# Four tokens in nine of batch 0's q are loaded first, and the rest follows behind v

## The chip, the cores and the metric

The kernel runs on one core of a Trainium2 chip. The metric is the device time of one execution in microseconds, the median of several runs.

## The reference

```python
def _attn_ref(q, k, v):                    # q, k, v: (8, 8, 576, 64) float32
    def phi(x):
        return np.where(x > 0, x, np.exp(x) - 1.0) + 1.0
    q_p, k_p = (phi(q), phi(k))
    kv = np.einsum('bhsd,bhse->bhde', k_p, v)
    z = np.sum(k_p, axis=2)
    num = np.einsum('bhsd,bhde->bhse', q_p, kv)
    den = np.einsum('bhsd,bhd->bhs', q_p, z)[..., None] + 1e-06
    return num / den

def _moe_ref(x, w_in, w_out, beta):        # x: (4608, 512), d_ff = 2048
    h = x @ w_in
    g = h * (1.0 / (1.0 + np.exp(-beta * h)))
    return g @ w_out
```

Linear attention over 8 batches of 8 heads comes first. Its output, transposed to (4608, 512), goes through a two-matrix layer with a Swish whose slope is beta. phi is computed as min(exp(x), max(x, 0) + 1).

## The kernel before

Work goes batch by batch (576 tokens each). A batch's tokens lie as 64 groups of J = 9 consecutive tokens; heads come in pairs. After transposition they make tiles of 128 rows: tiles t = 0 to 3 hold tokens 2t and 2t + 1 of every group, and tile 4 holds the ninth token (64 rows). Tiles 0 to 3 of a batch make the 512 columns of one pass through the layer. The ninth tokens of all batches are gathered in `xT_tail` and make a ninth pass at the end.

For each batch, in order:

- `phi_exp` (ScalarE), `phi_relu` and `phi_min` (VectorE) make phi of q and k, in two halves `pr`.
- q is transposed on TensorE for batches 0 and 1 (`q_half`, `q_last`, then `q_copy` out of PSUM to `qT`).
- `kv_both` makes k'v with a column of ones that gives z. Batch 0 has its own version: `z_sums`, `kv_first`, `kv_mask`, `zbd`, `dps`.
- `numer` (batch 0: `numer_first`, with the denominators from `denom`) makes num and divides; the result is `xs_sb`. `x_trans` (batch 0: `x_first`) transposes it to `xT`.
- The layer: `h_mm` makes one of 16 blocks `ff` of h in PSUM (`h_ps`), `silu` takes it to `g`; `y_mm(b, t, i)` adds the quarter `i` of the hidden units to tile `t` of y.

Batch 0's first four blocks of h are made tile by tile (`h_first(t)`, 16 matmuls of 128 columns each), as soon as each tile of `xT` is there. Blocks 4 to 15 are made at full width. Batch 0's y is made by 16 `y_mm` calls, and between them the attention part of batch 1 is placed: its q transposes, `kv_both(1)`, `numer(1, t)` and `x_trans(1, t)`. From batch 2 on a later batch's attention is placed inside `h_phase` and `y_fast`, where a product is saved by sums of blocks.

The order on each engine is the order in which the program text issues instructions (`manual_schedule`); each engine works through its own list in order and waits on semaphores. `idle(n)` issues n matmuls on a constant tile and nothing uses their result. `table(func)` makes ScalarE load the table of a function ahead of its use.

Loads: SyncE's queue gets the four halves of batch 0's q and k, float32, into parts of `stage` and `xk[0]` (`x0f`). All else comes through GpSimd's queue, in program order, with conversion to bf16 where the tile is bf16: v of batch 0 (`v0b`), four quarters of `w_in`, `w_out` 0 and 1 (float32, into the memory of `g_sb[1]`), q and k of batch 1, `w_out` 2 (into `stage`), v of batch 1, `w_out` 3, q and k of batch 2. GpSimd starts with a one-element copy `gate` that reads the end of q's first half, so that its loads begin when that half has landed:

```python
load(nc.sync, x0f[0], q, 0, 0, 2)
load(nc.sync, x0f[1], q, 0, 2, 2)
load(nc.sync, x0f[2], k, 0, 0, 2)
load(nc.sync, x0f[3], k, 0, 2, 2)
...
nc.gpsimd.tensor_copy(gate, x0f[0][:, 1, J - 1, D - 1 : D])
```

At most eight of GpSimd's loads are under way: the ninth waits for the first to land, and so on.

Of the kernel before, what the change touches and what calls it, by code (L numbers as in the profile page):

```python
# [16 lines left out]
def kernel(  # L17
# [65 lines left out]
    x3f = xk[0].rearrange("p i j d -> p (i j d)").bitcast(F32)  # L83
    x0f = [
        a.rearrange("p (i j d) -> p i j d", i=2, j=J)
        for a in [stage[:, n * 1152 : (n + 1) * 1152] for n in range(3)] + [x3f]
    ]
    v0b = vf.rearrange("p i j d -> p (i j d)").bitcast(BF16)[:, 0:2304].rearrange(
        "p (i j d) -> p i j d", i=4, j=J
# [6 lines left out]
    ws = [consts.tile([P, 8, HM], BF16, name=f"ws{i}") for i in range(4)] if FAST else None  # L96


    def load(eng, dst, src, b, i0=0, n=4):
        return eng.dma_start(  # L100
            out=dst.rearrange("p i j d -> p i (j d)"),
            in_=src[b].rearrange("(i a) (g j) d -> (a g) i (j d)", a=2, j=J)[:, i0 : i0 + n],
        )


    beta_row = consts.tile([FC, P], F32)
    nc.scalar.dma_start(out=beta_row, in_=moe_beta.rearrange("(c p) -> c p", p=P))
    load(nc.sync, x0f[0], q, 0, 0, 2)
    load(nc.sync, x0f[1], q, 0, 2, 2)
    load(nc.sync, x0f[2], k, 0, 0, 2)  # L110
    load(nc.sync, x0f[3], k, 0, 2, 2)
    nc.vector.memset(warm, 0.5)
    act0 = consts.tile([P, 1], F32, name="act0")
    nc.scalar.activation(act0, warm[:, 0:1], ACTF.Exp)
# [8 lines left out]
    nc.gpsimd.tensor_copy(gate, x0f[0][:, 1, J - 1, D - 1 : D])  # L123
    load(nc.gpsimd, v0b[:, 0:2], v, 0, 0, 2)
    load(nc.gpsimd, v0b[:, 2:4], v, 0, 2, 2)

    w_in_v = moe_w_in.rearrange("(c p) f -> p c f", p=P)
    w_out_v = moe_w_out.rearrange("(c p) m -> p c m", p=P)
    for i in range(4):
        nc.gpsimd.dma_start(out=w_in_sb[i], in_=w_in_v[:, :, i * 512 : (i + 1) * 512])  # L130

    def load_w_out(i):
        nc.gpsimd.dma_start(out=w_out_f[i], in_=w_out_v[:, i * 4 : (i + 1) * 4, :])

    load_w_out(0)
    load_w_out(1)
# [14 lines left out]
    def idle(n):  # L151
        for _ in range(n):
            nc.tensor.matmul(warm_ps, warm[:, 0:P], warm, start=True, stop=True)

    def table(func):
        nc.scalar.activation(act0, warm[:, 0:1], func)  # L156
# [128 lines left out]
    def rows_of(t):  # L285
        return P if t < NT - 1 else G
# [192 lines left out]
    qtp = [bank1("qtp", [P, 1024], BF16) for _ in range(2)]
    phi_part(0, "q", 0)  # L480
    q_half(0, 0, qtp[0])
    idle(3)
    phi_part(0, "q", 1)
    q_half(0, 1, qtp[1])
    t8 = bank1("qtp8", [P, 2 * P], BF16)
    q_last(0, t8)
# [3 lines left out]
    x = xin(0, "k", 0)  # L490
    phi_exp(0, "k", 0, x)
    phi_relu(0, "k", 0, x)
    q_copy(nc.vector, 0, 0, qtp[0])
    phi_min(0, "k", 0)
# [34 lines left out]
    z_sums(0)
    idle(1)  # L530
    phi_part(0, "k", 1)
    q_copy(nc.scalar, 0, 1, qtp[1])
    q_copy_last(nc.scalar, 0, t8)
    nc.scalar.copy(beta_s, bps)
    table(ACTF.Silu)
    kv_first(0)
    z_sums(1)
    idle(1)
    kv_mask(0)
    for hh in range(2):  # L540
        nc.vector.tensor_mul(
            zbd[:, hh], zps[hh][:, 0:2, None].to_broadcast([P, 2, 2]), kvmask[:, :, :, 0]
        )
    dps = bank("dps", [P, NT, 2, 2, 2])
    den0 = consts.tile([P, NT, 8], F32)
    rden0 = consts.tile([P, NT, 8], F32)
    for t in range(NT):
        n = rows_of(t)
        for hh in range(2):
            for pr in range(2):  # L550
                nc.tensor.matmul(
                    dps[:n, t, hh, pr], st[0, "qT"][:, pr, t, hh, 0:n], zbd[:, hh, pr, :],
                    start=True, stop=True, skip_group_check=True,
                )
    dv = dps.rearrange("p t a b c -> p t (a b c)")

    def denom(r, ts):
# [3 lines left out]
    kv_first(1)  # L561
    denom(P, slice(0, NT - 1))
    kv_mask(1)

    def numer_first(t):
# [8 lines left out]
        nc.vector.tensor_mul(
            xs_tile(0, t),
            nps[:n].rearrange("p a b (c d) -> p a (b c) d", d=D),
            rden0[:n, t].rearrange("p (a i) -> p a i", a=2)[:, :, :, None].to_broadcast(
                [n, 2, 4, D]
            ),
        )  # L580

    def x_first(t, eng):
        x_trans(0, t, eng, bank1("xtp0", [P, KC, P], BF16))


    hp0 = []

# [325 lines left out]
```

## Time and profile before

| | |
|---|---|
| median of 3 runs | 278.42 us (278.1 to 278.65) |
| the profiled execution: time | 277.78 us |
| its span, first to last instruction | 276.0 us |
| TensorE busy | 267.8 us (97%) |
| TensorE weight load, VectorE, ScalarE, GpSimd busy | 61%, 61%, 62%, 17% |
| read from and written to memory | 36.71 MB, 9.44 MB |

The times in the profile are from the start of the span. In its rows PE is TensorE's matmuls, PEld its weight loads, DVE is VectorE, ACT is ScalarE, POOL is GpSimd and SP is SyncE. L404 is line 404 of the kernel before; L153 is a matmul of `idle`, L163 to L175 are phi, L239 and L241 copies, L386 the transposes of `x_trans`, L404 is `h_mm`, L412 `silu`, L419 `y_mm`, L223 the matmuls of `kv_both`. A row of the timeline has start, duration, engine, line, operation, tiles, shape, number of instructions, and in brackets how long the engine was idle before and what ended that.

### The profile page before, as it was taken

What the parts mean: (1) busy time and instruction counts of PE and PEld (TensorE: products, weight loads), DVE (VectorE), ACT (ScalarE), POOL (GpSimd) and SP (SyncE); (2) the same over time, 40 slices, a digit from 0 to 9 for tenths busy, and PEclk for the clock granted to TensorE, in tenths of its full rate; (3) what the DMA queues carried; (4) which work ended last, traced back from release to release, by engine and by line L of the source; (5) the groups of instructions that cost most, each with busy time, mean ns of one, the idle gap of its engine ahead of it and who ended that gap; (6) DMA issues with size and microseconds to landing.
All of it is one profiled execution on the core that took longest, in us unless ns stands there. A gap on an engine that the chain in (4) does not pass through costs nothing.

```text
span 276.0 us, 6367 instructions
## 1 busy us (share of the span) xinstructions
PE 267.8 (97%) x2688; PEld 167.6 (61%) x2697; DVE 169.7 (61%) x329; ACT 170.1 (62%) x232; POOL 45.6 (17%) x60
## 2 busy tenths in 40 slices
PE   7899999999999999999999999999999999999994
PEld 2575455444445487548754885488548845874683
DVE  4771585967956997568857884779473414342532
ACT  4838887966915794579457945794573077117610
POOL 5922011042123040303030403040000000000000
PEclk9999999999999999999999999999999999999999
DMA  6999999569969946996799659956531040022013
GB/s 231 254 206 352 255 387 250 177 109 192 297 109 189 312 65 109 196 289 78 102 201 289 81 89 209 296 79 88 154 66 22 13 141 0 0 68 87 0 40 114
DMA packets 49228, 42.76 MB, mean 155 GB/s; under 512 B 30752, under 2 KB 41008, under 8 KB 49200
## 3 DMA queue, kind: packets, MB, share of 16 engines
q0 software_dynamic: 13040, 23.40, 36.4%
q1 hardware_dynamic: 35984, 18.82, 32.3%
q8 instruction: 21, 0.34, 0.5%
q10 hardware_dynamic: 176, 0.14, 0.2%
q14 instruction: 7, 0.06, 0.1%
HBM read 36.71 MB, written 9.44 MB: 167 GB/s over the span
## 4 chain that ended last, share of the span: by engine, by line
PE 82%; DMA 13%; DVE 1%; POOL 1%; issue 1%; ACT 0%; DVEq 0%; POOLq 0%
PE h_ps L404 41%; PE yb L795 9%; PE ya L795 9%; PE yd L795 9%; DMA vf<-in_v_dram 8%; PE y_ps L419 6%; PE yc L795 4%; DMA w_in<-in_moe_w_in_dram 4%; PE kvp L223 2%; PE nps L331 2%; DMA stage<-in_q_dram 1%; POOL vf L100 1%; PE nps L298 1%; DVE xs_sb L311 1%; ACT vaug L239 0%
## 5 line engine op out<-in xcount | busy, mean ns | idle before, releaser
L412 ACT ACTIVATE g<-h_ps,beta_c 128x512 bf16<-128x512 f32 x144 | 97.8, 688 | 69.1 <-PE h_ps L404 69.1
L404 PE MATMUL h_ps<-xT,w_in 128*128 128x512 bf16 (+1 forms) x560 | 114.5, 361 | 0.1
L404 PEld LDWEIGHTS <-w_in 128*128 128x128 bf16 x624 | 57.4, 98 | 62.3 <-issue 0.2
L795 PEld LDWEIGHTS <-stage 128*128 128x128 bf16 x448 | 43.8, 98 | 5.2
L795 PEld LDWEIGHTS <-g 128*128 128x128 bf16 x336 | 32.9, 98 | 5.3
L241 POOL CAST vaug<-vf 128x1152 bf16<-128x1152 f32 x13 | 18.4, 1443 | 74.7 <-DMA vf<-in_v_dram 74.7
L419 PE MATMUL y_ps<-w_out,g 128*128 128x512 bf16 x122 | 28.4, 379 | 0.4 <-issue 0.2
L795 PE MATMUL ya<-w_out,g 128*128 128x256 bf16 x224 | 26.7, 273 | 0.0
L725 DVE TENSOR_TENSOR stage<-g 128x1024 bf16<-128x1024 bf16 x14 | 9.6, 686 | 22.8 <-ACT g L412 22.8
L729 DVE TENSOR_TENSOR stage<-g 128x1024 bf16<-128x1024 bf16 x14 | 9.7, 691 | 19.2 <-ACT g L412 19.2
L346 DVE TENSOR_TENSOR xs_sb<-nps,rden 128x448 bf16<-128x448 f32 (+3 forms) x30 | 20.7, 689 | 1.0
L419 PEld LDWEIGHTS <-g 128*128 128x128 bf16 x128 | 12.2, 98 | 13.5
L163 ACT ACTIVATE e<-xk 128x1152 bf16<-128x1152 bf16 (+1 forms) x15 | 16.7, 1159 | 0.3 <-DMA xk<-in_k_dram 0.3
L163 ACT ACTIVATE e<-xq 128x1152 bf16<-128x1152 bf16 x14 | 15.6, 1160 | 0.0
L175 DVE TENSOR_TENSOR phi_k<-e,r 128x1152 bf16<-128x1152 bf16 x16 | 13.5, 850 | 1.4
L156 ACT ACT_TABLE_LOAD x11 | 14.1, 1283 | 0.2
L404 PE MATMUL h_ps<-xT_tail,w_in 128*128 128x512 bf16 x62 | 13.9, 379 | 0.1
L795 PE MATMUL yd<-ws,stage 128*128 128x256 bf16 x112 | 13.4, 273 | 0.0
L795 PE MATMUL yb<-ws,stage 128*128 128x256 bf16 x112 | 13.4, 272 | 0.0
L795 PE MATMUL yc<-ws,stage 128*128 128x256 bf16 x112 | 13.4, 273 | 0.0
L795 PE MATMUL yd<-ws,g 128*128 128x256 bf16 x112 | 13.4, 273 | 0.0
L795 PE MATMUL yb<-w_out,stage 128*128 128x256 bf16 x112 | 13.4, 272 | 0.0
(98 smaller groups left out, 233.8 us busy)
## 6 DMA issues: line engine op xcount, KB each, us to landing
vf<-in_v_dram POOLq DMA_DIRECT2D x7, 1152.0 KB, 13.3
out_dram<-y SPq DMA_DIRECT2D x25, 256.0 KB, 3.8
xq<-in_q_dram POOLq DMA_DIRECT2D x7, 576.0 KB, 8.3
xk<-in_k_dram POOLq DMA_DIRECT2D x7, 576.0 KB, 10.9
out_dram<-y SPq DMA_DIRECT2D x17, 128.0 KB, 2.9
w_in<-in_moe_w_in_dram POOLq DMA_DIRECT2D x4, 512.0 KB, 11.8
g<-in_moe_w_out_dram POOLq DMA_DIRECT2D x2, 1024.0 KB, 17.4
stage<-in_moe_w_out_dram POOLq DMA_DIRECT2D x2, 1024.0 KB, 21.6
```

The costliest lines, as they stand in the source:

```text
L156: nc.scalar.activation(act0, warm[:, 0:1], func)
L163: nc.scalar.activation(e, x, ACTF.Exp)
L175: nc.vector.tensor_tensor(st[b, a][:, pr].rearrange("p j (h d) -> p j h d", h=2), st[b, a, pr, "e"].rearrange("p h j d -> p j h d"), st[b, ...
L223: nc.tensor.matmul(t[half(il), a, pr * EA : (pr + 1) * EA], st[b, "k"][half(a), pr, j, il * D : (il + 1) * D], vaug[b % 2][half(a), pr, j, ...
L241: eng.tensor_copy(dst, src)
L346: nc.vector.tensor_mul(xs_sb[:n, ils, v0 * D : v1 * D].rearrange("p i (u d) -> p i u d", d=D), pv[:, :, :, 0:D], rden[:, :, :, None].to_br ...
L404: nc.tensor.matmul(hp[:, c0:c1].rearrange("p (t n) -> p t n", n=P), w_in_sb[ff // 4][:, kc, (ff % 4) * P : (ff % 4 + 1) * P], xm, start=(k ...
L412: nc.scalar.activation(g_sb[b % 2][:, ff, :], hp, ACTF.Silu, scale=beta_c[:, ff : ff + 1])
L419: nc.tensor.matmul(yp[:, c0:c1], g_sb[b % 2][:, ff, t * P : (t + 1) * P], w_out_sb[i][:, c, c0:c1], start=(ff == 0), stop=(ff == FC - 1), ...
L725: nc.vector.tensor_sub(gs[2][:, c], g[:, c, 0:HM], g[:, c, HM:512])
L729: nc.vector.tensor_add(gs[0][:, c], g[:, c, HM:512], g[:, c2, HM:512])
L795: nc.tensor.matmul(ps[:, p * HM : (p + 1) * HM], lhs(c, p), rhs(c), start=(first and (p == 0 or apart) and c == 0), stop=True, skip_group_ ...
```

## The change

Batch 0's q comes in two parts. The first four tokens of every group (tiles 0 and 1) are loaded first on SyncE's queue, as float32, in two pieces; then k in two halves. The other five tokens come as bf16 into `xq[0]` by GpSimd's queue, behind v. w_in's first quarter is loaded in two halves behind that. `w_out` 3 is loaded in two pieces.

The program order of batch 0's head is rewritten for it. phi and the transposes of tokens 0 to 3 (`Part`, `q_first(0)`, `q_first(1)`) stand ahead of k. Tiles 0 and 1 go as far as `h_first(0)`; phi of the other tokens stands between; then come `q_first(2)`, `q_first(3)`, `q_last`, and the denominators, numerators, transposes and `h_first` of tiles 2 to 4. The load of Silu's table moves from before `kv_first(0)` to behind the copy of `x_first(1)`. In batch 0's y, `y_mm(0, 2, 2)` moves ahead of `kv_both(1)`, `y_mm(0, 3, 2)` ahead of `numer(1, 0)` and `y_mm(0, 0, 3)` ahead of `x_trans(1, 0)`.

```diff
-    load(nc.sync, x0f[0], q, 0, 0, 2)
-    load(nc.sync, x0f[1], q, 0, 2, 2)
-    load(nc.sync, x0f[2], k, 0, 0, 2)
-    load(nc.sync, x0f[3], k, 0, 2, 2)
+    for pr in range(2):
+        load(nc.sync, x0q[pr], q, 0, 2 * pr, 2, 0, 4)
+    for pr in range(2):
+        load(nc.sync, x0k[pr], k, 0, 2 * pr, 2)
...
-    nc.gpsimd.tensor_copy(gate, x0f[0][:, 1, J - 1, D - 1 : D])
+    nc.gpsimd.tensor_copy(gate, x0q[0][:, 1, 3, D - 1 : D])
     load(nc.gpsimd, v0b[:, 0:2], v, 0, 0, 2)
     load(nc.gpsimd, v0b[:, 2:4], v, 0, 2, 2)
+    load(nc.gpsimd, xq[0][:, :, 4:J], q, 0, 0, 4, 4, 5)
...
-    for i in range(4):
-        nc.gpsimd.dma_start(out=w_in_sb[i], in_=w_in_v[:, :, i * 512 : (i + 1) * 512])
+    for i, c0, c1 in ((0, 0, 256), (0, 256, 512), (1, 0, 512), (2, 0, 512), (3, 0, 512)):
+        nc.gpsimd.dma_start(
+            out=w_in_sb[i][:, :, c0:c1], in_=w_in_v[:, :, i * 512 + c0 : i * 512 + c1]
+        )
...
-    idle(11)
+    idle(9)
...
+    def q_first(t, eng):
+        tp = bank1("qtp", [P, 512], BF16)
+        for pr in range(2):
+            for jj in range(2):
+                nc.tensor.matmul(
+                    tp.rearrange("p (r h i g) -> p r h i g", r=2, h=2, i=2)[:, pr, :, jj, :],
+                    st[0, "q"][:, pr, 2 * t + jj, :], identity,
+                    is_transpose=True, start=True, stop=True, skip_group_check=True,
+                )
+        copy(
+            eng, st[0, "qT"][:, :, t].rearrange("p r h n -> p r (h n)"),
+            tp.rearrange("p (r x) -> p r x", r=2),
+        )
...
+    qa = [Part(x0q[pr], 2 * pr, 0) for pr in range(2)]
+    for p in qa:
+        p.exp()
+        p.relu()
+        p.min()
+    q_first(0, nc.vector)
+    q_first(1, nc.scalar)
     bps = bank("bps", [P, FC])
     nc.tensor.matmul(bps, beta_row, ident16, is_transpose=True, start=True, stop=True)
-    idle(4)
...
+    idle(3)
...
+    phi_part(0, "k", 0)
+    z_sums(0)
+    idle(2)
+    phi_part(0, "k", 1)
+    nc.scalar.copy(beta_s, bps)
+    z_sums(1)
+    kv_first(0)
...
+    dps = bank("dps", dps_shape)
+    den_mm(dps, (0, 1))
+    kv_mask(0)
+    denom(dps, P, slice(0, 2))
+    kv_first(1)
+    kv_mask(1)
+    qb = [Part(xq[0][:, 2 * pr : 2 * pr + 2, 4:J], 2 * pr, 4) for pr in range(2)]
+    qb[0].exp()
+    for t in range(2):
+        numer_mm0(t)
+    for t in range(2):
+        numer_xs0(t)
     x_first(0, nc.scalar)
-    numer_first(3)
+    qb[1].exp()
+    for p in qb:
+        p.relu()
+        p.min()
+    h_first(0)
     x_first(1, nc.scalar)
-    h_first(0)
-    numer_first(4)
+    table(ACTF.Silu)
+    q_first(2, nc.vector)
+    q_first(3, nc.scalar)
+    t8 = bank1("qtp8", [P, 2 * P], BF16)
+    q_last(0, t8)
+    q_copy_last(nc.vector, 0, t8)
+    h_first(1)
+    dps = bank1("dps", dps_shape)
+    den_mm(dps, (2, 3, 4))
+    numer_mm0(2)
+    numer_mm0(3)
+    denom(dps, P, slice(2, 4))
+    numer_xs0(2)
+    numer_xs0(3)
     x_first(2, nc.scalar)
-    h_first(1)
+    h_first(2)
+    denom(dps, G, slice(4, 5))
+    numer_mm0(4)
+    numer_xs0(4)
     x_first(3, nc.scalar)
...
-    h_first(2)
+    h_first(3)
     x_first(4, nc.vector)
-    h_first(3)
...
-    load_w_out(3)
+    load_w_out(3, 2)
...
-    for t in range(2):
+    for t in range(3):
         y_mm(0, t, 2, yps[t])
     kv_both(1)
...
-    y_mm(0, 2, 2, yps[2])
+    y_mm(0, 3, 2, yps[3])
     numer(1, 0)
-    y_mm(0, 3, 2, yps[3])
     numer(1, 1)
+    y_mm(0, 0, 3, yps[0])
     x_trans(1, 0, nc.scalar)
     phi_exp(2, "q", 0, xin(2, "q", 0))
-    y_mm(0, 0, 3, yps[0])
```

`Part` holds phi of one part of q: `exp` on ScalarE, `relu` and `min` on VectorE. `den_mm`, `numer_mm0` and `numer_xs0` are the matmuls and the division of `dps` and `numer_first`, taken apart by tile.

More of the change, by code (lines that the diff above doesn't have):

```diff
@@ L82 @@
     ]
[L83 to L86, printed above, removed]
+    x0k, x0q = [
+        [
+            stage[:, c + n * 2 * nj * D : c + (n + 1) * 2 * nj * D].rearrange(
+                "p (i j d) -> p i j d", i=2, j=nj
+            )
+            for n in range(2)
+        ]
+        for c, nj in ((0, J), (2304, 4))
     ]
@@ L96, with load @@
     ws = [consts.tile([P, 8, HM], BF16, name=f"ws{i}") for i in range(4)] if FAST else None
-    def load(eng, dst, src, b, i0=0, n=4):
+    def load(eng, dst, src, b, i0=0, n=4, j0=0, nj=J):
         return eng.dma_start(
             out=dst.rearrange("p i j d -> p i (j d)"),
-            in_=src[b].rearrange("(i a) (g j) d -> (a g) i (j d)", a=2, j=J)[:, i0 : i0 + n],
+            in_=src[b].rearrange("(i a) (g j) d -> (a g) i (j d)", a=2, j=J)[
+                :, i0 : i0 + n, j0 * D : (j0 + nj) * D
+            ],
         )
@@ L122, with load_w_out @@
     gate = consts.tile([P, 1], BF16)
-    nc.gpsimd.tensor_copy(gate, x0f[0][:, 1, J - 1, D - 1 : D])
+    nc.gpsimd.tensor_copy(gate, x0q[0][:, 1, 3, D - 1 : D])
     load(nc.gpsimd, v0b[:, 0:2], v, 0, 0, 2)
     load(nc.gpsimd, v0b[:, 2:4], v, 0, 2, 2)
+    load(nc.gpsimd, xq[0][:, :, 4:J], q, 0, 0, 4, 4, 5)
     w_in_v = moe_w_in.rearrange("(c p) f -> p c f", p=P)
     w_out_v = moe_w_out.rearrange("(c p) m -> p c m", p=P)
-    for i in range(4):
-        nc.gpsimd.dma_start(out=w_in_sb[i], in_=w_in_v[:, :, i * 512 : (i + 1) * 512])
-    def load_w_out(i):
-        nc.gpsimd.dma_start(out=w_out_f[i], in_=w_out_v[:, i * 4 : (i + 1) * 4, :])
+    for i, c0, c1 in ((0, 0, 256), (0, 256, 512), (1, 0, 512), (2, 0, 512), (3, 0, 512)):
+        nc.gpsimd.dma_start(
+            out=w_in_sb[i][:, :, c0:c1], in_=w_in_v[:, :, i * 512 + c0 : i * 512 + c1]
+        )
+    def load_w_out(i, n=4):
+        for c in range(0, 4, n):
+            nc.gpsimd.dma_start(
+                out=w_out_f[i][:, c : c + n], in_=w_out_v[:, i * 4 + c : i * 4 + c + n, :]
+            )
     load_w_out(0)
@@ L183, in xin @@
         if b == 0:
-            return x0f[pr if a == "q" else 2 + pr]
+            return x0k[pr]
         return (xk if a == "k" else xq)[b % 2][:, 2 * pr : 2 * pr + 2]
@@ L474, with __init__, exp, relu @@
     beta_s = consts.tile([P, FC], F32)
+    class Part:
+        def __init__(self, x, i0, j0):
+            self.x, self.i0, self.j0 = x, i0, j0
+            self.n, self.nj = x.shape[1], x.shape[2]
+            self.e, self.r = [
+                work.tile([P, 2, J, D], BF16, tag=s, name=s, bufs=4).rearrange(
+                    "p i j d -> p (i j d)"
+                )[:, 0 : self.n * self.nj * D].rearrange("p (i j d) -> p i j d", i=self.n, d=D)
+                for s in ("e", "r")
+            ]
+        def exp(self):
+            nc.scalar.activation(self.e, self.x, ACTF.Exp)
+        def relu(self):
+            nc.vector.tensor_scalar(self.r, self.x, 0.0, 1.0, ALU.max, ALU.add)
+        def min(self):
+            for i in range(0, self.n, 2):
+                nc.vector.tensor_tensor(
+                    st[0, "q"][:, (self.i0 + i) // 2, self.j0 : self.j0 + self.nj].rearrange(
+                        "p j (h d) -> p j h d", h=2
+                    ),
+                    self.e[:, i : i + 2].rearrange("p h j d -> p j h d"),
+                    self.r[:, i : i + 2].rearrange("p h j d -> p j h d"),
+                    ALU.min,
+                )
+    def q_first(t, eng):
[6 more added lines that the diff above has]
+                    is_transpose=True, start=True, stop=True, skip_group_check=True,
+                )
+        copy(
+            eng, st[0, "qT"][:, :, t].rearrange("p r h n -> p r (h n)"),
+            tp.rearrange("p (r x) -> p r x", r=2),
+        )
     phi_tile(0, "q")
@@ L478 @@
     q_tile(0)
[L479 to L486, printed above, removed]
+    qa = [Part(x0q[pr], 2 * pr, 0) for pr in range(2)]
[5 more added lines that the diff above has]
+    q_first(1, nc.scalar)
     bps = bank("bps", [P, FC])
     nc.tensor.matmul(bps, beta_row, ident16, is_transpose=True, start=True, stop=True)
-    idle(4)
[L490 to L494, printed above, removed]
+    idle(3)
     zps = [bank("zps") for _ in range(2)]
@@ L527, in kv_mask, with den_mm, denom, numer_mm0 @@
             )
[L529 to L544, printed above, removed]
+    dps_shape = [P, NT, 2, 2, 2]
     den0 = consts.tile([P, NT, 8], F32)
     rden0 = consts.tile([P, NT, 8], F32)
[L547 to L557, printed above, removed]
+    def den_mm(dps, ts):
+        for t in ts:
+            n = rows_of(t)
+            for hh in range(2):
+                for pr in range(2):
+                    nc.tensor.matmul(
+                        dps[:n, t, hh, pr], st[0, "qT"][:, pr, t, hh, 0:n], zbd[:, hh, pr, :],
+                        start=True, stop=True, skip_group_check=True,
+                    )
+    def denom(dps, r, ts):
+        dv = dps.rearrange("p t a b c -> p t (a b c)")
         nc.vector.tensor_scalar(den0[:r, ts], dv[:r, ts], 1e-6, None, ALU.add)
         nc.vector.reciprocal(rden0[:r, ts], den0[:r, ts])
[L561 to L565, printed above, removed]
+    def numer_mm0(t):
         n = rows_of(t)
-        nps = bank1("nps0", [P, 2, 2, P])
+        nps = st[0, "nps", t] = bank1("nps0", [P, 2, 2, P])
         for hh in range(2):
@@ L573, in numer_first, with numer_xs0 @@
                 )
+    def numer_xs0(t):
+        n = rows_of(t)
         nc.vector.tensor_mul(
             xs_tile(0, t),
-            nps[:n].rearrange("p a b (c d) -> p a (b c) d", d=D),
+            st[0, "nps", t][:n].rearrange("p a b (c d) -> p a (b c) d", d=D),
             rden0[:n, t].rearrange("p (a i) -> p a i", a=2)[:, :, :, None].to_broadcast(
@@ L592, in h_first @@
             h_mm(xT[0], ff, hp0[ff], t * P, (t + 1) * P)
-    for t in range(3):
-        numer_first(t)
-    denom(G, slice(NT - 1, NT))
-    x_first(0, nc.scalar)
-    numer_first(3)
-    x_first(1, nc.scalar)
-    h_first(0)
-    numer_first(4)
+    phi_part(0, "k", 0)
[5 more added lines that the diff above has]
+    kv_first(0)
+    for hh in range(2):
+        nc.vector.tensor_mul(
+            zbd[:, hh], zps[hh][:, 0:2, None].to_broadcast([P, 2, 2]), kvmask[:, :, :, 0]
+        )
+    dps = bank("dps", dps_shape)
[10 more added lines that the diff above has]
+        numer_xs0(t)
+    x_first(0, nc.scalar)
+    qb[1].exp()
[3 more added lines that the diff above has]
+    h_first(0)
+    x_first(1, nc.scalar)
+    table(ACTF.Silu)
[12 more added lines that the diff above has]
+    numer_xs0(3)
     x_first(2, nc.scalar)
-    h_first(1)
+    h_first(2)
+    denom(dps, G, slice(4, 5))
+    numer_mm0(4)
+    numer_xs0(4)
     x_first(3, nc.scalar)
```

## The prediction

> **What bounds the kernel now.** I read the table by engine and the chain of waits first. TensorE is busy 97% of the span, and from 44 us on the chain is nearly all its matmuls at 0.216 us each. So the total can move only through what happens before: when TensorE gets to the second batch's `h_ps` (51.16 us). In the chain of waits (start, duration, what) the head is this:
>
> ```profile
> 0.74 3.68 DMA stage<-in_q_dram
> 4.48 0.78 POOL gate L123
> ...
> 7.63 10.85 DMA w_in<-in_moe_w_in_dram
> 18.52 0.52 issue
> 19.04 21.56 DMA vf<-in_v_dram
> 40.62 1.16 ACT vaug L239
> 41.83 0.84 PE kvp L223 x71
> ```
>
> It names transfers: batch 1's v lands at 40.60, is cast, and `kv_both(1)` starts at 41.83. But that is only the last comer. The stretches (PE busy, PEld, DVE, ACT, POOL, clock, DMA share, GB/s) say that TensorE had no room either:
>
> ```profile
> 14.00:17.00 3.00, 2.37 (x32) 1.76 (x31) 2.63 (x9) 0.95 (x2) 0.75 (x1) 1.00 1.24 207
> 17.00:20.00 3.00, 3.00 (x53) 2.81 (x51) 1.96 (x7) 1.26 (x3) 0.76 (x1) 1.00 1.24 205
> 20.00:31.50 11.50, 11.50 (x75) 5.91 (x73) 3.86 (x9) 9.42 (x16) 2.25 (x3) 1.00 1.13 296
> 31.50:41.50 10.00, 9.89 (x59) 4.91 (x58) 6.79 (x14) 8.53 (x9) 0.84 (x1) 1.00 1.06 362
> 41.50:51.00 9.50, 8.69 (x131) 4.97 (x132) 6.57 (x18) 8.03 (x12) 1.06 (x2) 1.00 1.03 253
> ```
>
> From 17 to 41.5 TensorE is full, and it waits about 0.2 us for v. Two limits lie side by side, TensorE's own row from 16.67 and the DMA stream (share over 1 throughout). A change that loses TensorE time after 16.67 loses it for good; one that gains there gains at most 0.2 us before v stops it. The timeline gives the pieces (start, duration):
>
> ```profile
> 12.01 1.28 ACT L156 ACT_TABLE_LOAD   x1
> ...
> 15.60 0.40 PE L386 MATMUL xtp<-identity,xs_sb 128*128 128x128 bf16 x4 [0.34 <-DVE xs_sb L574]
> ...
> 16.03 1.19 ACT L239 COPY xT<-xtp 128x512 bf16<-128x512 bf16 x2 [2.52 <-PE xtp L386]
> ...
> 16.67 1.05 PE L404 MATMUL h_ps<-xT,w_in 128*128 128x128 bf16 x16
> ```
>
> These are the table load (hidden before kv), tile 0's transposes, two ACT copies of 0.59 us, and `h_first(0)`, 1.05 us.
>
> **Step 1, the head moves forward.** q and k wait 576 KB per half (q landed at 4.43 and 6.35, k at 8.11 and 9.56, the starts or waits of their readers). Now 512 KB of q precede k instead of 1152. The stream moves about 0.39 KB per ns (window of 36 to 40 us: 388 GB/s), so k and v0 come 640/0.39 = 1.6 us sooner: k at 6.5 and 7.9, v0 at 9.7 and 11.1 (was 11.3 and 12.7). `kv_first(1)` started at 13.35; now it can at 11.5, behind `den_mm`. From it to `h_first(0)` the chain took 16.67 - 13.35 = 3.3 us and keeps its parts, so `h_first(0)` could start at 14.8: 1.9 us sooner. ACT's two small exponentials and the small relus lie before k lands and cost nothing; if k came before them, some 0.6 us each.
>
> **Step 2, w_in.** The same bytes of q, k and v stand ahead of w_in's first quarter as before, only in another order. It landed at 6.74 + 8.5 = 15.24 (issue plus the shortest landing time of `w_in`). The half with ff 2 and 3 cannot land sooner. The extra packets, 512 of q and 512 of w_in, are 64 on each of 16 engines. The profile shows no 1 KB reads under load. Lower end: the stream pays by bytes read, and the q that is written as bf16 is 0.33 MB less to write, at most -0.8 us at 0.39; upper end: 22 ns each, what the packet records give for a 4-byte one, 1.4 us. Since 1152-byte results of 2304-byte reads went at 178 packets per us and uncast 2304-byte ones at 177, time goes by reads: I take +0.2, so 15.5. Then `h_first(0)` runs ff 0 and 1 at 14.8, waits, and ends at 15.5 + 0.05 + 0.53 = 16.1 (before: 17.72). Here the new kernel is 1.6 us ahead.
>
> One rule speaks against the halves. Row: the four quarters, 1 MB read each, landed some 2.5 to 3.2 us apart, which is bytes over 0.39 and little else. The Trainium skill, "DMA: Bandwidth & Descriptors", section "Anatomy of one DMA", prices each DMA at about 2.0 us fixed plus bytes/436e3, so an extra piece would cost 2 us. By that the total would be 2 us higher; I go by the row, in which a queued DMA shows no such charge.
>
> **Step 3, tiles 2 to 4 come late.** Before, all of q was transposed by 9, and from the end of `h_first(0)` (17.72) to ff 4, the first full-width `h_mm`, took 3.73 us: `y_ps` starts at 31.82, and 48 matmuls of 0.216 precede it, so ff 4 began at 21.45. Now five of nine tokens of q land where v did (12.7 to 13), and the program order on each engine after `h_first(0)` is a chain. ACT does: copy of xT(1), table load for Silu, copy of qT(3), copies of xT(2) and xT(3). TensorE waits in order for these. The sum, each from a row of before:
> - `x_first(1)` transposes to copy start 0.43, copy 0.59
> - table load 1.28 and its small activation 0.20, now ahead of qT(3) on ACT
> - `q_first(3)` copy, 512 columns, 0.59
> - `den_mm` of tiles 3 and 4, 8/20 of 0.77 and a hand-over: 0.36
> - `denom` 0.50 (0.19 and 0.35 for 32 columns, now 16)
> - `xs0(2)` 0.63 + 0.05; transposes to copy 0.43; copy 0.59 + 0.05
> - `h_first(2)` 1.05, `numer_mm0(4)` 0.25
> - `x_first(3)` 0.43 + 0.59 + 0.05; `h_first(3)` 1.05; `x_first(4)` 0.25
>
> This makes 9.4, and 9.5 with hand-overs. Only `h_first(1)` and the transposes `q_first(2)`, `q_first(3)` lie beside it. So ff 4 begins at 16.1 + 9.5 = 25.6, against 21.45: +4.15. Ff 4 to 15 stay 48 x 0.216, the w_in quarters are long there, and w_out 0 and 1 land at 26.7 and 29.4, ahead of their use.
>
> A second rule prices the load higher. Row: the load before the second batch's exponentials took 1.28, begins 0.02 after the last Silu and the next activation follows at once. "ScalarE: Activation LUTs", section "What ACT_TABLE_LOAD costs", adds a drain of about 1.38 us to the 1.28. By it the chain would be 1.4 longer; I take the row.
>
> **Step 4, Y0's kv later.** One `y_mm` of 4 x 0.216 = 0.87 moves from behind `kv_both(1)` to ahead of it. TensorE reaches kv at +10.0 after the end of batch 0's h now (41.83 - 31.82), of which 0.2 is the wait for v. It becomes 10.67: +0.66. What follows kv, up to `h_ps` at 51.16 (9.33 us), is set by the four `numer` tiles on VectorE (0.17, 0.20, 0.69 with gaps, 1.14 each) and by two PSUM buffers that each reader must free, not by the `y_mm` between. So nothing is given back; at best the 0.8 us idle of that stretch goes (gain 0.66). v, some 4 us early now, stops mattering. POOL's later loads wait for landings that come no later.
>
> **Sum.** +4.15 + 0.66 = 4.8; a few hand-overs may overlap, so I say 4.7. Against the profiled execution (span 276.0, time 277.78): span 280.7, time 282.5. The median of the runs is 278.42, 0.64 above, so 283.1. A difference under 0.2% (0.56 us) can't be told from none.
>
> **Rivals.**
> - Faster: the early half of q lets TensorE run dense. If the table load fell under `h_first(0)` and tiles 2 to 4 were ready by 16, the extra work there (q transposes, den, two numers, 1.8 us) would just eat the 1.9 us of step 1, ff 4 would start at 21.4, and kv, fed behind one more `y_mm`, would lose the 0.2 us wait and up to 0.8 idle after it: 277.5. For it: `h_first(0)` can start sooner. Against: it turns on whether qT(3) is copied before about 17, and ACT copies it behind xT(1) and the load. 0.05.
> - Smaller loss: part of the chain is hidden (the load, 1.5, or the 0.66 of step 4): 280.9 to 281.6. 0.11.
> - Larger loss: w_in's second half 1.4 late, or the clock falls. The warm-up matmuls of 512 columns took 0.43 each up to 5.27 and those of the later stages 0.216, so a half-rate stretch of three `h_first` costs 2 to 3 us: 285 to 286. For it: idle gaps of over 1 us between 7 and 9. 0.12.
> - k not sooner: v0 was issued at 5.19 and its first packets moved at 8.5. If that lag is POOL's own, the stream has a hole of up to 0.5 us before v0 and everything shifts by it: 283.6, inside my range. 0.04.
>
> **How the numbers follow.** My forecast has 0.68. Faster by over 0.2% is the first rival, 0.05; within it 0.02; slower 0.93. The range takes the packets' bounds (-0.8 hidden by TensorE's own readiness at 14.8, so -0.2, to +1.2), the hand-overs (-0.6) and the upper part of the smaller loss: 281.1 to 285.3.
>
> **What would show it.** Right: k's exponentials start near 6.6 and 8; `h_first(0)` begins near 14.8 with a wait inside; ACT's table load at 17 ahead of a qT copy; idle on TensorE of some 3 us between 16 and 25; ff 4 near 25.6; `kv_both(1)` near 46.6 with no wait for v; the second batch's `h_ps` near 55.9. Wrong: TensorE full from 16 to 22, or kv still waiting for v.

## The result and the profile after

| | before | after |
|---|---|---|
| median | 278.26 us (4 runs, 277.96 to 278.65) | 287.58 us (4 runs, 286.3 to 289.55) |
| profiled execution: time, span | 277.78, 276.0 | 287.42, 285.6 |
| ff 4 of batch 0 starts | 21.45 | 30.13 |
| `kv_both(1)`, `h_ps` of the second batch start | 41.83, 51.16 | 51.10, 60.43 |

The ratio is 1.034, interval 1.0279 to 1.0401: 9.3 us slower, where 4.7 were forecast and 285.3 was the end of the range. The direction was right, the size was not. Medians in this document are over all runs, while a ratio leaves out a run that took over 1.5% longer than the fastest of its kernel (one each in `e1_fill`, `e3_table`, `e4_again` and `e7_touch`), so differences between kernels are read from the ratios.

The stretches of the kernel after, in the same columns as before (PE busy, PEld, DVE, ACT, POOL, clock, DMA share, GB/s); the first two rows are new, the other five answer to the rows of before:

```profile
8.00:11.00 3.00, 0.00 (x0) 0.00 (x0) 1.44 (x2) 1.52 (x2) 2.37 (x3) 1.00 1.18 204
11.00:14.00 3.00, 2.61 (x56) 1.57 (x56) 1.82 (x5) 0.87 (x2) 1.05 (x2) 0.54 1.38 197
14.00:17.00 3.00, 2.85 (x38) 2.10 (x34) 1.67 (x7) 0.74 (x1) 1.51 (x3) 0.50 1.35 203
17.00:20.00 3.00, 1.97 (x18) 1.77 (x18) 2.64 (x6) 1.22 (x2) 1.19 (x2) 0.50 1.25 207
20.00:31.50 11.50, 8.52 (x111) 6.92 (x109) 5.32 (x17) 5.87 (x10) 3.45 (x5) 0.94 1.14 296
31.50:41.50 10.00, 10.00 (x48) 4.54 (x47) 4.01 (x10) 8.40 (x14) 0.24 (x1) 1.00 1.08 352
41.50:51.00 9.50, 9.39 (x57) 4.71 (x56) 5.24 (x10) 9.28 (x10) 1.91 (x2) 1.00 0.81 157
```

Two things stand here that the forecast did not have. TensorE did nothing between 8 and 11, and from 11 to past 20 its clock was half. A full-looking row can deceive: 14 to 17 is 2.85 of 3.00 busy, but at half clock. The third, the loss of TensorE time between 20 and 31.5 (8.52 of 11.50), was forecast. From 31.5 on TensorE is full, and the wait for v is gone (v landed at 42.01).

The chain of waits, its head (start, duration, what):

```profile
1.76 7.43 DMA stage<-in_k_dram
9.19 0.02 issue
9.21 1.17 ACT e L176
...
18.04 0.59 ACT xT L252
18.63 0.04 issue
18.68 1.87 PE h_ps L417 x16
20.54 0.44 PE xtp L399 x4
21.00 0.59 ACT xT L252
21.61 1.28 ACT L169
22.90 0.20 ACT act L169
23.11 0.48 ACT qT L252
```

It begins with k now, which landed at 9.19 instead of the forecast 6.5, and runs on through `h_first(0)` (18.68), the table load (21.61) and the copy of qT(3) behind it. The timeline shows how long TensorE stood, and where its work of the second part begins (start, duration, engine, line, ...; the bracket is the idle time before and what ended it):

```profile
11.22 0.40 PE L554 MATMUL zps<-ones,phi_k 64*128 64x1 bf16 x18 [3.95 <-DVE phi_k L188]
...
18.68 1.87 PE L417 MATMUL h_ps<-xT,w_in 128*128 128x128 bf16 x16 [0.67 <-ACT xT L252]
...
23.64 0.47 PE L589 MATMUL dps<-zbd,qT 128*128 128x2 bf16 x8 [0.83 <-ACT qT L252]
...
26.53 1.05 PE L417 MATMUL h_ps<-xT,w_in 128*128 128x128 bf16 x16 [0.67 <-ACT xT L252]
...
28.93 1.05 PE L417 MATMUL h_ps<-xT,w_in 128*128 128x128 bf16 x16 [0.67 <-ACT xT L252]
...
30.13 2.12 PE L417 MATMUL h_ps<-xT,w_in 128*128 128x512 bf16 x9
```

`h_first(0)` took 1.87 us, the two later ones 1.05 each: the same 16 matmuls at half and at full clock.

### The profile page after: what moved, and what is told of

It is laid out like the page before. It is cut to its first block, busy times and chain, and to the rows that moved or that the text cites. A ratio compares the mean times of both kernels' runs of the same rounds, so it can differ in the third digit from the quotient of the medians.

```text
span 285.6 us, 6372 instructions
## 1 busy us (share of the span) xinstructions
PE 269.7 (94%) x2683; PEld 169.1 (59%) x2691; DVE 171.4 (60%) x337; ACT 170.4 (60%) x234; POOL 46.7 (16%) x63
## 4 chain that ended last, share of the span: by engine, by line
PE 87%; DVE 4%; ACT 4%; DMA 3%; issue 1%; SPq 0%; DVEq 0%; ACTq 0%
PE h_ps L417 44%; PE y_ps L432 8%; PE yd L868 8%; PE yb L868 8%; PE ya L868 7%; PE yc L868 4%; DMA stage<-in_k_dram 3%; PE kvp L236 2%; PE nps L344 2%; ACT e L176 1%; ACT xT L252 1%; PE xtp L399 1%; ACT L169 1%; PE kvp L565 1%; DVE phi_q L188 1%
## 5 line engine op out<-in xcount | busy, mean ns | idle before, releaser
L417 PEld LDWEIGHTS <-w_in 128*128 128x128 bf16 x624 | 58.3, 99 | 64.5 <-issue 2.4
L188 DVE TENSOR_TENSOR phi_q<-e,r 128x1152 bf16<-128x1152 bf16 x14 | 12.1, 866 | 8.8 <-ACT e L176 7.6
L176 ACT ACTIVATE e<-xk 128x1152 bf16<-128x1152 bf16 x14 | 15.5, 1160 | 0.0
```

The source lines that it names most:

```text
L188: nc.vector.tensor_tensor(st[b, a][:, pr].rearrange("p j (h d) -> p j h d", h=2), st[b, a, pr, "e"].rearrange("p h j d -> p j h d"), st[b, ...
L417: nc.tensor.matmul(hp[:, c0:c1].rearrange("p (t n) -> p t n", n=P), w_in_sb[ff // 4][:, kc, (ff % 4) * P : (ff % 4 + 1) * P], xm, start=(k ...
```

## The experiments

Landing times below are those of the trace's semaphore events; "by bytes" is the landing of the queue's first piece plus what stands behind it at 0.39 KB per ns, as in step 1. All edits are against the kernel after, unless they say otherwise; microseconds are left out where plain.

**The kernel after again** (`e4_again`, no edit).

> The changed kernel itself, for a second profile. Theory C and rival D both leave open whether the lag of one DMA engine by 2.3 us in the first profile (k's first half: fifteen sixteenths by 6.9, the last at 9.2) belongs to the kernel or to that execution. If it belongs to the kernel, k's exponential starts again near 9.2 and the clock falls again; if to the execution, k lands by 7 and the time is 1 to 3 us less. Its four times were 286.3 to 289.55, so 287.5 is expected either way in the median.

287.67 (ratio 1.0285, 1.021 to 1.0359). Its profile has k at 8.20, the clock at half from 9.52 to 23.17, and 9.7 from the end of `h_first(0)` to ff 4. So the late k and the half clock are no accident of one execution.

### The clock

**TensorE kept busy while k is awaited** (`e1_fill`).

```diff
-    idle(3)
+    idle(16)
```

> The changed kernel with 16 instead of 3 matmuls on the constant tile ahead of k (3.5 us of work at 0.216 each), so that TensorE is not idle from 7.3 to 11.2. Theory A (two things were missed: the clock, which stood at 0.5 from 11.24 to 21.48 after that idle time, and k's late landing): the clock stays at 1.0; the kv, numer and transposes of tiles 0 and 1 and h_first(0) go at full speed, some 2.4 us less, so about 285. Rival B (the late landing of k and w_in alone sets the path, the half clock is hidden by waits): 287 to 287.6, unchanged.

285.71 (ratio 1.0241, 1.0181 to 1.03). By the ratios that is 1.2 less than `e4_again` on the same chip (1.0285, 1.021 to 1.0359). The intervals overlap, so the gain in time is not clear of noise; what the profile shows is the clock, which stayed at 1.0 from 6.95 to 17.19:

```profile
11.00:14.00 3.00, 2.65 (x66) 1.88 (x66) 1.85 (x9) 0.00 (x0) 1.51 (x2) 1.00 1.34 196
14.00:17.00 3.00, 1.49 (x19) 1.02 (x17) 2.49 (x6) 1.96 (x3) 1.50 (x2) 1.00 1.38 202
17.00:20.00 3.00, 2.18 (x21) 2.18 (x22) 0.55 (x2) 0.66 (x2) 0.76 (x1) 0.53 1.25 207
```

From k's first exponential to `h_first(0)` it took 16.12 - 7.82 = 8.3 us, exactly the forecast's 14.8 - 6.5; in the kernel after, at half clock, it was 9.47 (18.68 - 9.21). Not all of these 1.2 arrive in `h_first(0)`'s end, for w_in's second half now ends a wait inside it:

```profile
16.12 0.61 PE L417 MATMUL h_ps<-xT,w_in 128*128 128x128 bf16 x8 [0.67 <-ACT xT L252]
17.82 1.03 PE L417 MATMUL h_ps<-xT,w_in 128*128 128x128 bf16 x8 [1.09 <-DMA w_in<-in_moe_w_in_dram]
```

That is the wait that step 2 forecast, 2.3 us later than it forecast it.

**Fill, table load behind the copies, and the old order of y together** (`e12_three`): the edits of `e1_fill` and `e3_table`, and the `y_mm` calls as before:

```diff
-    for t in range(3):
+    for t in range(2):
         y_mm(0, t, 2, yps[t])
     kv_both(1)
...
-    y_mm(0, 3, 2, yps[3])
+    y_mm(0, 2, 2, yps[2])
     numer(1, 0)
+    y_mm(0, 3, 2, yps[3])
     numer(1, 1)
-    y_mm(0, 0, 3, yps[0])
     x_trans(1, 0, nc.scalar)
     phi_exp(2, "q", 0, xin(2, "q", 0))
+    y_mm(0, 0, 3, yps[0])
```

> The changed kernel with three of the losses taken out together: 16 matmuls on the constant tile ahead of k, the table load behind the copies of q_first, and batch 0's y_mm in the order of the kernel before. If the terms add up (clock 1.9 as measured, table 0.9 to 2.4 as measured, y_mm 0.4 to 0.8 as measured): 283.0 to 284.2, still slower than before by 5, which is the late k and the tiles 2 to 4 that wait for the rest of q. If one hides another: 285.

284.63 (ratio 1.0182, 1.0135 to 1.0229). `e10_dst`, measured beside it, is the kernel after but for two places in memory; against it this is 3.1 less by the ratios (each known to 1.3 to 1.6 either way) and 2.3 by the medians. The parts as measured would add up to 3.1 (1.2, 0.9 and 1.0). In its profile k came at 8.64 and the half clock had only moved: it held from 22.97 to 29.8, over the later `h_first`, which take 1.05 at full clock:

```profile
22.78 1.72 PE L417 MATMUL h_ps<-xT,w_in 128*128 128x128 bf16 x16 [0.67 <-ACT xT L252]
...
26.29 1.87 PE L417 MATMUL h_ps<-xT,w_in 128*128 128x128 bf16 x16 [0.67 <-ACT xT L252]
```

From the end of `h_first(0)` (18.01) to ff 4 (28.41) it took 10.40 here and 8.76 in `e3_table`, so about 1.6 of the 5 us that remain were still the clock in this profile. By the sums of the traces the rest is the late k and the chain of tiles 2 to 4; no run takes these two apart.

**The kernel before with four more idle matmuls** (`e18_bfill`, against before), between q's halves and ahead of k.

```diff
-    idle(3)
+    idle(4)
     phi_part(0, "q", 1)
...
-    idle(4)
+    idle(7)
     x = xin(0, "k", 0)
```

> The kernel before with four more idle matmuls: four instead of three between the two halves of q, seven instead of four ahead of k. In the profile of one earlier variant of the kernel before (the y matmuls moved) TensorE stood idle 0.91 us ahead of k and 0.53 ahead of q's second half, and the clock was half from 13.4 to 20.2. By the theory that such gaps bring the half clock, filling them keeps the clock at 1.0, and the executions of 279 to 280 us become rarer: median 277.4 to 278.2, up to 0.3% below the kernel before. Rival: the gaps do not matter, or the matmuls get in the way where k lands early (4 x 0.216 = 0.9 us, of which 0.65 lie in the wait for v): 278.2 to 278.7, no difference.

278.62 against 278.81 (ratio 0.9992, 0.9969 to 1.0016): no difference. Its profile kept the full clock from 6.46 on, and the executions above 279.5 were 1 of 12 against 3 of 17, too few to tell.

### Steps 2 to 4 by themselves

**The table load behind the q copies** (`e3_table`).

```diff
     x_first(1, nc.scalar)
-    table(ACTF.Silu)
     q_first(2, nc.vector)
     q_first(3, nc.scalar)
     t8 = bank1("qtp8", [P, 2 * P], BF16)
     q_last(0, t8)
     q_copy_last(nc.vector, 0, t8)
+    table(ACTF.Silu)
```

> The changed kernel with the load of Silu's table behind the copies of q_first(2), q_first(3) and q_last in the program order, so that ScalarE copies qT(3) ahead of it. My chain has the load and its activation as a term of 1.48 us: 286.1, with den_mm of tile 3 no longer waiting for ScalarE and ff 4 starting about 1.4 us sooner. Rival: the load is hidden by h_first(1) and other waits, under 0.5 us.

285.23 (ratio 1.0213, 1.0158 to 1.0268). The chain from the end of `h_first(0)` (18.63) to ff 4 (27.39) fell to 8.76 from 9.6 or 9.7. The load and its activation are 1.48; moving them gave back 0.8 to 0.9. In this profile k also landed earlier, at 7.27. That is 1.92 before the 9.19 of the kernel after, and `h_first(0)` ended 1.92 earlier (18.63 against 20.55): between these two profiles the landing of k passes on in full to the end of `h_first(0)`. By the ratios the time is 2.0 below `e4_again`, with intervals that overlap.

**Step 4 alone** (`e5_ymm`, against before): the diff of `e12_three`'s `y_mm` calls the other way round, as in the change.

> The kernel before with only the change in batch 0's y: y_mm(0, 2, 2) ahead of kv_both(1), y_mm(0, 3, 2) ahead of numer(1, 0), y_mm(0, 0, 3) ahead of x_trans(1, 0). My step 4: kv_both starts 0.66 later and nothing comes back after it, so 0.66 longer, 278.9 to 279.1 against 278.3. Rival: the move fills TensorE's wait for v and is worth its idle time, 0.2 to 0.9 shorter.

279.04 (before 278.22, 12 and 29 runs; ratio 1.0036, 1.0005 to 1.0067): 1.0 us, between 0.1 and 1.9. In the profile, from the end of batch 0's h to `kv_both(1)` it took 10.59 (forecast 10.67), and from there to `h_ps` 9.27 (9.33): nothing is given back.

**w_in's first quarter in halves, alone** (`e6_halves`, against before).

```diff
-    for i in range(4):
-        nc.gpsimd.dma_start(out=w_in_sb[i], in_=w_in_v[:, :, i * 512 : (i + 1) * 512])
+    for i, c0, c1 in ((0, 0, 256), (0, 256, 512), (1, 0, 512), (2, 0, 512), (3, 0, 512)):
+        nc.gpsimd.dma_start(
+            out=w_in_sb[i][:, :, c0:c1], in_=w_in_v[:, :, i * 512 + c0 : i * 512 + c1]
+        )
```

> The kernel before with only w_in's first quarter loaded in two halves. By the rows (a queued load pays for its bytes) no change within 0.2%: 278.2 to 278.6. Rival, a fixed cost of about 2 us for each load: v lands 2 us later and kv waits for it, up to 280.3.

278.54 against 278.22 (ratio 1.0000, 0.9973 to 1.0027). The piece more costs nothing that can be seen (the interval is 0.8 us either way), as the row of before said. The 2 us fixed per DMA of the Trainium skill, "DMA: Bandwidth & Descriptors", section "Anatomy of one DMA", do not show in this queue of pieces.

### Why k came late

In the kernel after, the packet records show single packets of k that took 0.5 to 2 us, where the median of its 2304-byte packets is 0.093; the 16 DMA engines lagged unevenly: 15 of them had k's first half by 6.90, the last at 9.19. The stretch from 3.6 to 8 us of the kernel after, and then of the kernel before, has in its last column that the core moved 268 GB/s, and 350 before:

```profile
3.60:8.00 4.40, 3.03 (x17) 1.17 (x15) 2.09 (x5) 1.85 (x3) 4.19 (x7) 1.00 0.94 268
```

```profile
3.60:8.00 4.40, 4.27 (x18) 1.79 (x16) 2.89 (x4) 2.33 (x2) 3.52 (x5) 1.00 1.01 350
```

**GpSimd's loads issued only when k is there** (`e2_gate`).

```diff
-    nc.gpsimd.tensor_copy(gate, x0q[0][:, 1, 3, D - 1 : D])
+    nc.gpsimd.tensor_copy(gate, x0k[0][:, 1, J - 1, D - 1 : D])
```

> The changed kernel with GpSimd's gate reading the end of k's first half instead of q's first piece, so that v and the rest are issued after k's first half has landed. Theory C (GpSimd's early loads, their descriptors or packets, hold up k on SyncE's queue): k lands near 6.5 and 8 instead of 9.2 and 10.6, the clock does not fall, v0 lands no later than in the changed kernel: about 283 to 285. Rival D (k is held up by something of its own, its first reads or a lagging DMA engine): k lands at 8 to 9 again, v0 some 3 us later than before, time 289 or more.

289.37 (ratio 1.036, 1.0308 to 1.0413). k landed at 8.68 and the long packets were there, with no load of GpSimd's under way. The early issue of GpSimd's loads is not the cause; v0 at 13.34 and 16.07 is what the later gate cost.

**Whole rows of q first** (`e9_qrows`): the first two loads take all nine tokens, as before, the rest of the change stays.

```diff
-    x0k, x0q = [
...
-        for c, nj in ((0, J), (2304, 4))
+    x0full = [
+        s.rearrange("p (i j d) -> p i j d", i=2, j=J)
+        for s in (stage[:, 2304:3456], xk[0].rearrange("p i j d -> p (i j d)").bitcast(F32))
+    ]
+    x0q = [s[:, :, 0:4] for s in x0full]
...
-        load(nc.sync, x0q[pr], q, 0, 2 * pr, 2, 0, 4)
+        load(nc.sync, x0full[pr], q, 0, 2 * pr, 2)
```

> The changed kernel with q's first load as in the kernel before: whole rows of nine tokens, 2304 bytes a packet, of which the first four are used (so 0.66 MB more stands ahead of k and 0.66 MB of q is read twice). Theory P (the 1 KB packets of q, 1 KB out of each 2304, put the 16 DMA engines into a state in which k's packets stall): long packets at k's start are as few as in the kernel before, k's first half lands at 7.8 to 8.2 although 1.6 us of bytes more stand ahead of it, and the time is 285 to 287.5, no worse than the changed kernel. Rival Q (k's packets stall for another reason): k lands 1.6 us later than in the changed kernel, near 10, and the time is 1.5 us longer, 289.

288.51 (ratio 1.0336, 1.0282 to 1.039); k at 9.07, between the two landings that were expected, and 1.4 later than by bytes, with long packets. So long packets come without 1 KB reads. Whether 1 KB reads add to them stays open: the packets of over 0.3 us that start behind 2.5 us on SyncE's queue sum to 7.5 us here and 7.4 in the kernel before, and to 10.6 in the kernel after and 18.6 in `e10_dst`, but to 6.0 in `e1_fill`, which has 1 KB reads too.

**Places in `stage` exchanged** (`e10_dst`).

```diff
-        for c, nj in ((0, J), (2304, 4))
+        for c, nj in ((1024, J), (0, 4))
```

> The changed kernel with the places in the stage tile exchanged: q's pieces at words 0 to 1023 and k behind them, as in the kernel before, where k stood behind q. Theory W (writes of k into the part of the tile that it has now collide with something): k lands near 6.5, time 285 to 286. Rival: the place is of no account, k lands at 7.3 to 9.2, 287.5.

286.92 (ratio 1.0294, 1.0238 to 1.035); k at 8.24, as late as before the exchange, with long packets. The place where k is written is not the cause.

**A first touch of k** (`e7_touch`, and `e8_btouch` on the kernel before): a load of 64 single values of k on ScalarE's queue ahead of the others.

```diff
+    touch = consts.tile([64, 1], F32, name="touch")
+    nc.scalar.dma_start(
+        out=touch, in_=k[0].rearrange("h (a s) d -> (h a) (s d)", a=8)[:, 0:1]
+    )
```

> The changed kernel with one small extra load at the start on ScalarE's queue: one float32 of each of 64 stretches of batch 0's k, 18 KB apart. In all profiles so far single packets of 0.5 to 2 us appear on SyncE's queue just when k's first packets start (3.6 to 6.5 in the changed kernels, 5.2 to 6.2 in the one before). Theory F (the first reads of a tensor are slow, whatever asked for them): the small load takes that cost early, k lands near 6.5 and 8, 1 to 2.5 us off the time, so 285 to 286.5. Rival: the long packets belong to the load itself (its queue, its writes, its time): k lands at 7.3 to 9.2 as before, 287.5.

> The kernel before with the same small extra load of k. Theory F: the slow packets at 5.2 to 6.2 go, k lands 0.4 to 0.5 sooner and all transfers behind it too; the time falls by 0 to 0.5 us, as TensorE's own row is full. Rival: no change in k's landing (8.1 and 9.6), 278.3.

287.0 (ratio 1.0289, 1.0234 to 1.0343), k at 7.58 with long packets; and 277.87 (ratio 0.9994, 0.997 to 1.0018). `e8_btouch` had only two packets of over 0.3 behind 2.5 us (0.30 and 0.43), but `e6_halves`, which touches nothing, had none. The touch explains nothing.

**No engine reads q while k comes** (`e13_kread`, and its halves `e14_act`, where ScalarE alone reads q, and `e15_dve`, where VectorE alone does): phi and the transposes of q's first part are moved behind k's, one run each.

```diff
-    for p in qa:
-        p.exp()
-        p.relu()
-        p.min()
-    q_first(0, nc.vector)
-    q_first(1, nc.scalar)
...
     phi_part(0, "k", 1)
+    for p in qa:
+        p.exp()
+        p.relu()
+        p.min()
...
+    q_first(0, nc.vector)
+    q_first(1, nc.scalar)
```

In `e14_act` the `p.exp()` stay in their place, in `e15_dve` the `p.relu()`.

> The changed kernel with phi of q's first part placed behind phi of both halves of k, so that ScalarE and VectorE read nothing of the stage tile until k has landed; the loads are unchanged. Theory R (the engines' reads and writes beside the loads make packets long): no long packets from 3.5 to 6.5, k lands near 6.2 and 7.6. Rival S (k's reads behind q's are slow by themselves): long packets as before, k lands at 7.3 to 9.2. The time is not of interest (q's part comes later).

> As e13, but ScalarE's two exponentials of q's first part stay ahead of k; VectorE's relu and min of it come behind k. Under theory R with ScalarE as the cause: long packets from 3.6 on, k at 7.3 or later; with VectorE as the cause: none, k near 6.2. Under rival S: long packets in e13, e14 and e15 alike.

> As e13, but VectorE's two relus of q's first part stay ahead of k; ScalarE's exponentials and the min come behind k. Under theory R with VectorE as the cause: long packets from 3.6 on, k at 7.3 or later; with ScalarE as the cause: none, k near 6.2. Under rival S: long packets in all three.

289.58, 288.95 and 290.81; k at 8.67, 8.77 and 8.56, with long packets in all three. The engines' reads are not the cause.

**k ahead of q on SyncE's queue** (`e11_kfirst`, one run).

```diff
-    for pr in range(2):
-        load(nc.sync, x0q[pr], q, 0, 2 * pr, 2, 0, 4)
     for pr in range(2):
         load(nc.sync, x0k[pr], k, 0, 2 * pr, 2)
+    for pr in range(2):
+        load(nc.sync, x0q[pr], q, 0, 2 * pr, 2, 0, 4)
```

> The changed kernel with k's two loads ahead of q's two pieces on SyncE's queue; ScalarE and VectorE still take q first, so its time says nothing and only the packets are looked at. Theory P: with k's packets first there are no long packets before q's pieces start, and the two halves of k land at 4.4 and 6. Rival Q, long packets come at a certain time after the start (3.6 to 6.5) whatever is under way: k's second half lands at 6.5 or later, with long packets among it.

291.77. k landed at 4.56 and 6.06 and q's parts at 7.20 and 7.90, each some 0.5 later than by bytes, with hardly a long packet (three of 0.3 to 0.4 us behind 2.5 us). So it is not k's data. Why the total is worse is not taken apart: the gate still waits for q, v0 came at 11.54 and 15.42 (11.99 and 13.42 in the kernel after), and the clock was half from 7.74 to 24.81 and from 28.22 to 35.05.

**The kernel before again** (`e16_before`, one run, no edit).

> The kernel before, a second look at its packets. It tells how regular the long packets at 4.8 to 6.3 are there: in its first profile they cost k 0.5 us, in two profiles of kernels with the same start (e6, e8) there were none. Under theory R they are there whenever q's exponential starts while k's packets flow, which it does here too (4.4 to 4.8), so k at 8.1; under rival S they come and go, k at 7.8 to 8.9.

278.41. k landed at 9.15, one engine far behind the others. Late pieces occur in the kernel before too.

**The kernel before with k first** (`e17_kq`, against before). The `gate` reads the end of k's first half.

```diff
-    load(nc.sync, x0f[0], q, 0, 0, 2)
-    load(nc.sync, x0f[1], q, 0, 2, 2)
     load(nc.sync, x0f[2], k, 0, 0, 2)
     load(nc.sync, x0f[3], k, 0, 2, 2)
+    load(nc.sync, x0f[0], q, 0, 0, 2)
+    load(nc.sync, x0f[1], q, 0, 2, 2)
...
+    phi_part(0, "k", 0)
     z_sums(0)
-    idle(1)
+    idle(4)
     phi_part(0, "k", 1)
+    z_sums(1)
+    phi_part(0, "q", 0)
+    idle(4)
+    q_half(0, 0, qtp[0])
+    phi_exp(0, "q", 1, xin(0, "q", 1))
...
+    kv_first(0)
+    q_half(0, 1, qtp[1])
```

> The kernel before, with k's two loads ahead of q's on SyncE's queue and the head's program order following them: phi and z of k first, then phi of q, its transposes, and kv. Theory S says that long packets come when k is read behind q; with k ahead they did not come in the one look at the changed kernel, so here k should land by 4.6 and 6.2, q by 7.7 to 8.2 and 9.2 to 9.7, v0 not later than 12.7, and no packet of the first queue longer than 0.4 us. Then the last copy of qT ends near 12.7, where the matmuls of the denominators now begin near 12.65, and the time is that of the kernel before, 277.6 to 278.6, at most 0.5 lower where the kernel before loses time to late packets. Rival: the second tensor on the queue is what is slow, whichever it is; then q lands at 8 and 9.5 to 10.5, qT is 0.3 to 1 us late, and the time is 278.6 to 279.6.

280.63 against 278.22 (11 and 16 runs; ratio 1.0082, 1.0059 to 1.0106). k landed at 4.60 and 6.09, with one long packet (0.46 at 2.21); q's first half at 8.71, 1.2 later than by bytes, with long packets from 5.7 on. So what is late is not k as such, but what stands third on the queue. The rival's price was too low by 1.0: the half clock came too, from 16.68 to 20.09, over `h_first(0)`.

Taken together, the third piece on SyncE's queue landed later than by bytes in nearly every profile:

| | third piece at | by bytes | late |
|---|---|---|---|
| before, `e16_before`, `e5_ymm`, `e6_halves`, `e18_bfill` (k) | 8.11, 9.15, 8.94, 7.84, 8.80 | 7.4 to 7.8 | 0.1 to 1.5 |
| `e8_btouch` (k) | 7.85 | 7.8 | 0.1 |
| `e9_qrows` (k), `e17_kq` (q) | 9.07, 8.71 | 7.7, 7.6 | 1.4, 1.2 |
| after, `e1_fill`, `e3_table`, `e4_again`, `e10_dst`, `e12_three` (k) | 9.19, 7.80, 7.27, 8.20, 8.24, 8.64 | 5.7 to 5.9 | 1.5 to 3.3 |
| `e2_gate`, `e7_touch`, `e13_kread`, `e14_act`, `e15_dve` (k) | 8.68, 7.58, 8.67, 8.77, 8.56 | 5.7 to 5.8 | 1.8 to 3.1 |
| `e11_kfirst` (q) | 7.20 | 6.7 | 0.5 |

With 640 KB less ahead of it, k landed at 7.3 to 9.2, before at 7.8 to 9.2: the landing hardly followed the bytes. What makes the packets long stays open. As a cause by itself each of these is excluded: GpSimd's loads, 1 KB reads of q, the place of k in SBUF, a first touch, readers on ScalarE and VectorE, and k as such.

## Why the prediction was right in direction and wrong in size

**Step 1 failed.** "k and v0 come 640/0.39 = 1.6 us sooner: k at 6.5 and 7.9" is a sum of bytes at the stream's rate of a later window (36 to 40 us, from GpSimd's queue). The pieces on SyncE's queue between 3.6 and 8 did not go at that rate: k landed at 9.19 and 10.62, 2.7 late. The rows for it were in the trace of before: the core moved 401 GB/s from 4 to 5 us and 210 from 5 to 6, and k's own piece was 0.7 later than by bytes. The forecast took that as a constant of the landing, not as something that could grow. The rival "k not sooner" named GpSimd's queue and 0.5 us for it; the place was wrong and the price too small.

**Step 2 was late by what it inherited.** w_in's second half landed at 17.73, not 15.5. From k's second landing to it 7.1 us went by, where the forecast's times have 15.5 - 7.9 = 7.6 (`e4_again` 7.4, `e3_table` 7.3, `e1_fill` 8.6). And in `e6_halves` the extra piece cost nothing that can be seen.

**Left out of the sum: the clock.** It stood as a rival, at 0.12, with 2 to 3 us, "for it: idle gaps of over 1 us". The late k made one gap of 3.95, and the clock was half from 11.24 to 21.48. Against the forecast that cost 1.2 up to `h_first(0)` (9.47 for 8.3) and 0.6 inside it (1.87 for 1.3, which held a wait for w_in). The first of the two is gone in `e1_fill`, where the time fell by 1.2, not clear of noise. The rival's mechanism was right and its price near (1.8 for 2 to 3), though the half clock lay over the kv, the numerators and one `h_first`, not over three. Whether the clock would have fallen with k at 6.5 no run shows. The gap would have been some 1.3 (11.22 - 9.19 + 6.5 - 7.27), but the clock fell with k at 7.27 too (`e3_table`, half from 9.68 to 19.92), and in `e5_ymm` with no gap over 0.91.

**Step 3 was right.** From the end of `h_first(0)` to ff 4: 9.5 forecast, 9.58 in the profile, 9.7 in `e4_again`. The order of its terms is the one seen (xT(1) copied 21.00, load 21.61, qT(3) 23.01, `den_mm` 23.64, xT(2) 25.89, xT(3) 28.29). One term was too large as a term that can be taken out: the load's 1.48 are on the chain, but `e3_table` got only 0.8 to 0.9 of them back.

**Step 4 was right.** 0.66 forecast; 10.6 and 9.33 in the profile against 10.67 and 9.33, and +1.0 (0.1 to 1.9) as a run of its own.

The sum, as measured on the spans: 4.8 forecast, + 2.7 (k) + 1.2 (half clock ahead of `h_first(0)`) + 0.6 (in it) + 0.1 (step 3) + 0.2 (step 4 and after) = 9.6, which is 285.6 - 276.0. Of the signs given for right, the table load ahead of a qT copy, an idle TensorE (2.98 between 20 and 31.5) and `kv_both(1)` without a wait for v came; k's exponentials near 6.6 did not, and all the times behind them were shifted. The faster rival turned on qT(3) being copied before about 17; it was copied at 23.01.

## What to carry to other kernels

Bytes ahead of a transfer over the stream's rate give the soonest it can land, not when it lands: look how each piece of the same queue landed against its bytes in the trace before, and let the range reach to "no sooner at all". When a change empties TensorE's list ahead of a load, price the late load together with the half clock that its idle gap can bring, not as a rival beside it. A chain of waits summed row by row from the trace of before held within 0.1 us over 9.5; its starting point was the weak part.

## What the runs showed of the hardware

- The stretches of half clock lasted whole multiples of about 3.41 us: 10.24 in the kernel after (11.24 to 21.48), 13.65 in `e4_again`, 17.07 in `e2_gate`, 3.42 in `e1_fill` and `e17_kq`.
- It needs no long idle gap. In `e1_fill` it came at 17.19 after a stretch in which TensorE was busy 1.49 of 3.00 us; the gaps ahead of it were 0.56 and 0.67, and one of 1.09 was under way. In `e5_ymm` no gap was over 0.91. The Trainium skill, "TensorE: Matmul & The Clock Gate", section "What's actually happening", has windows of about 3.4 us, which agrees with the multiples, and one idle window as what brings the half clock; here a half-busy one was enough.
- The busy share of TensorE alone does not tell when it comes. Two stretches of 3.41 us were equally busy (lines below, the first from `e4_again`, the second from `e12_three`); the full clock went on behind the first and ended with the second. What decides stays open.
- The 16 DMA engines of one queue drifted apart by more than 2 us (15 were done by 6.90, the last at 9.19, with k's first half), and the piece has landed only with the slowest.

```profile
23.17:26.58 3.41, 1.94 (x30) 1.61 (x28) 1.98 (x6) 0.59 (x1) 0.93 (x2) 1.00 1.07 387
```

```profile
19.56:22.97 3.41, 1.94 (x36) 1.61 (x34) 1.98 (x6) 1.88 (x3) 0.90 (x2) 1.00 1.24 209
```
